# Four batches' y taken together in chunks 2 to 5, and the first quarter of w_in loaded as two column blocks, in a fused retention and GELU kernel

## The chip, the cores and the metric

The kernel runs on one core of a Trainium2 chip. The time is device microseconds of the whole kernel, from its first instruction to its last. It was measured at 217.58 us for the kernel before, the median of three runs (217.08 to 217.91).

A core has a matmul engine (TensorE, PE in the profile), two engines for elementwise work that can read the matmul results in PSUM (VectorE, DVE; ScalarE, ACT), a third [...](GpSimd, POOL), and a sequencer that only issues transfers (SyncE, SP). ScalarE and GpSimd issue transfers too. Every engine runs its own instructions in order and waits for others by semaphores.

## What is computed

The reference is a retention layer followed by a feed-forward layer. It is cut here to what matters:

```python
# attention: 4 batches, 8 heads, 768 steps, head size 64
gamma = 1.0 - 2.0 ** (-5.0 - np.arange(H))
for t in range(S):
    state = gamma * state + k[:, :, t] (outer) v[:, :, t]
    y[:, :, t] = 1/sqrt(D) * q[:, :, t] @ state
# feed-forward: x is y as (4 * 768 tokens) x 512
h = x @ w_in                       # 512 x 2048
g = 0.5 * h * (1 + tanh(c * (h + 0.044715 * h**3)))
out = g @ w_out                    # 2048 x 512
```

All inputs and the output are float32. The kernel casts to float16 for its matmuls.

## The kernel before

The kernel cuts the 768 steps into six chunks of 128 steps, numbered 0 to 5. In a chunk the recurrence becomes matmuls. With q and k scaled by powers of gamma, each batch needs:

- T: the transposes of q and k (in chunk 0 and 1 by TensorE; in chunk 2 only k by TensorE; from chunk 3 on neither: VectorE does them in blocks);
- A = k q, masked to the past, two PSUM banks per batch (64 rows of the array each);
- y = state times q ("yc"), plus v times A ("yi", 64 columns of the array each), one bank per batch;
- S = k v, which is added to the decayed state for the next chunk.

All four batches of a chunk are then one block of 512 tokens for the feed-forward layer: 16 units h (4 matmuls of 512 columns each, then a GELU on ScalarE), and 16 units o (4 matmuls of 512 columns each). While the units of chunk c run, the small matmuls of chunk c + 1 are put between them. Below, q3 means q of batch 3 in the chunk spoken of, and likewise for k and v.

The first loads. SyncE, ScalarE and GpSimd each have a queue:

```python
    nc.sync.dma_start(out=cst[:, :OKT + 16], in_=cst_h.ap())
    load1(nc.scalar, "q", 0, 0)
    load1(nc.sync, "k", 0, 0)
    load1(nc.scalar, "k", 0, 1)
    load1(nc.sync, "q", 0, 1)
    load1(nc.scalar, "v", 0, 0)
    load1(nc.sync, "v", 0, 1)
    load1(nc.sync, "k", 0, 2)
    load1(nc.sync, "q", 0, 3)
    load1(nc.sync, "v", 0, 3)
```

The scaling of one tensor, on the engine that is given:

```python
    def prep1(eng, nm, c, b):
        t = pre.tile([128, H, Dh], F16, ...)
        src = ld_tile(nm, c, b)
        if nm == "v":
            ...                                  # a cast
        else:
            eng.tensor_tensor(out=t, in0=src, in1=cst[...], op=ALU.mult)
```

PSUM has eight banks. They are given out in turn, under three tags:

```python
    BANKS = {"h": 2, "o": 2, "att": 4}

    def bank(tag, dt=F32, shape=(128, NHP, 128), name="ps"):
        return psum.tile(list(shape), dt, tag=tag, bufs=BANKS[tag], name=name)
```

The y of a pair of batches, with the A of another pair between its two parts:

```python
    def att_AY(c, bs, tag, ca, abs_, eng):
        for b in bs:
            mm_yc(c, b, tag)
        for b in abs_:
            mm_A(ca, b)
        for b in bs:
            mm_yi(c, b)
        ...                                      # ev_A and ev_Y: the copies out of PSUM
```

The first quarter of w_in comes in two halves by rows (kc 0, 1 and kc 2, 3), in a cast from float32 to float16 on the way:

```python
    NI = 4
    w_in_part = [(0, 0, 2), (0, 2, 4)] + [(i, 0, NHP) for i in range(1, NI)]
    w_in_sb = [
        const.tile([128, k1 - k0, NF // NI * 128], F16, name=f"w_in{i}_{k0}")
        for i, k0, k1 in w_in_part
    ]

    def w_in_of(fc, kc):
        i, r = fc // (NF // NI), fc % (NF // NI)
        t, k0 = (w_in_sb[i + 1], 0) if i else (w_in_sb[kc // 2], kc // 2 * 2)
        return t[:, kc - k0, r * 128:(r + 1) * 128]

    NO = 4
    w_out_sb = [const.tile([128, NF // NO, d_model], F16, name=f"w_out{i}") for i in range(NO)]

    def load_w_in(n):
        i, k0, k1 = w_in_part[n]
        nc.gpsimd.dma_start(
            out=w_in_sb[n],
            in_=moe_w_in.rearrange("(kc p) (i n) -> p kc i n", p=128, i=NI)[:, k0:k1, i],
        )
```

The start of the program, up to the point from which units of h and o run without a break (`spin` gives TensorE empty matmuls):

```python
    load1(AC, "q", 0, 2)
    load1(AC, "k", 0, 3)
    spin(14)
    prep1(VE, "q", 0, 0)

    load_w_in(0)
    prep1(PO, "k", 0, 0)
    mm_T(0, 0)
    ev_T(0, 0, AC)
    load1(AC, "v", 0, 2)
    prep1(VE, "q", 0, 1)
    prep1(PO, "k", 0, 1)
    load_w_in(1)
    prep1(PO, "k", 0, 2)
    for i in range(2, len(w_in_part)):
        load_w_in(i)
    prep1(PO, "k", 0, 3)
    for i in range(NO):
        load_w_out(i)
    spin(4)
    mm_A(0, 0)
    ev_A(0, 0)
    mm_T(0, 1)
    ev_T(0, 1, AC)
    prep1(AC, "v", 0, 0)
    spin(3)
    mm_A(0, 1)
    prep1(VE, "q", 0, 2)
    ev_A(0, 1)
    mm_yc(0, 0, "o")
    mm_yi(0, 0)
    ev_Y(0, 0, AC)
    mm_s(0, 0, "o")
    spin(3)
    prep1(AC, "v", 0, 1)
    mm_T(0, 2)
    ev_T(0, 2, AC)
    mm_yc(0, 1, "o")
    mm_yi(0, 1)
    ev_Y(0, 1, AC)
    ev_S(0, 0, AC)
    prep1(VE, "q", 0, 3)
    spin(5)
    mm_A(0, 2)
    ev_A(0, 2)


    t01, t2, t3 = (0, half), (half, half + C), (half + C, 2 * half)
    m1a = [moe1_parts(0, fp, *t01) for fp in range(2)]
    m1a[0](range(2))
    mm_T(0, 3)
    ev_T(0, 3, AC)
    m1a[1](range(2))
    mm_s(0, 1, "o")
    m1a[0](range(2, 4))
    mm_A(0, 3)
    ev_A(0, 3)
    prep1(VE, "v", 0, 2)
    m1a[1](range(2, 4))
    prep1(AC, "v", 0, 3)
    ev_S(0, 1, AC)
    mm_yc(0, 2, "o")
    mm_yi(0, 2)
    ev_Y(0, 2)
    mm_s(0, 2)
    mm_s(0, 3)
    mm_yc(0, 3, "o")
    mm_yi(0, 3)
    ev_Y(0, 3, AC)
    moe1_two(0, 0, *t2)
    moe1_two(0, 1, *t2, "o")
    moe1_two(0, 0, *t3)
    moe1_two(0, 1, *t3, "o")
```

The loads of chunk 1 (`hold` writes one element of the target when a part of w_out has landed, so that the loads behind it start no sooner), and the units between which chunk 1 is put:

```python
    hold("q", 1, 1, w_out_sb[2][0:1, 0, 0:1])
    for fc in range(4, NF):
        moe1(0, fc)
        if fc in (9, 11, 13):
            load1(AC, "qkk"[(fc - 9) // 2], 1, fc // 13)
    ...
    def preps(c, b):
        prep1(VE, "q", c, b)
        prep1(PO, "k", c, b)

    for nm, b in (("q", 1), ("q", 2), ("v", 0), ("q", 3), ("k", 3), ("v", 1), ("v", 2), ("v", 3)):
        load1(SY, nm, 1, b)
    load1(AC, "k", 1, 2)
    u = [units2(0, b, tag="ooho"[b]) for b in range(B)]
    run(
        [u[i % 3][i // 3] for i in range(12)] + u[3],
        {
            8: [(preps, 1, 0)],
            10: [(att_T, 1, 0), (preps, 1, 1)],
            11: [(prep1, AC, "v", 1, 0), (att_AY, 1, (), "att", 1, (0,), None)],
            12: [(prep1, AC, "v", 1, 1), (att_T, 1, 1), (preps, 1, 2)],
            13: [(att_AY, 1, (0,), "h", 1, (1,), AC)],
            14: [(prep1, AC, "v", 1, 2), (att_T, 1, 2), (preps, 1, 3), (att_S, 1, 0)],
            15: [
                (prep1, AC, "v", 1, 3),
                (att_AY, 1, (1,), "h", 1, (2,), AC),
                (att_T, 1, 3),
                (att_S, 1, 1),
            ],
        },
    )
```

The plan for chunk 2, and for chunks 3 to 5 (n = c + 1). The number is the unit behind which a piece stands:

```python
        {
            ...
            8: [(att_T, 2, 0), (load, 3)],
            10: [(att_T, 2, 1)],
            13: [(att_AY, 1, (), "o", 2, (0, 1), None)],
            14: [(att_T, 2, 2)],
            15: [(att_T, 2, 3)],
        },
    run(
        [x for b in range(B) for x in units2(1, b)],
        {
            2: [(att_AY, 2, (0, 1), "h", 2, (2, 3), AC)],
            4: [(att_S, 2, 0)],
            5: [(att_S, 2, 1)],
            8: [(att_AY, 2, (2, 3), "h", 2, (), AC)],
            10: [(att_S, 2, 2)],
            11: [(att_S, 2, 3)],
        },
    )


    for c in range(2, NCk - 1):
        n = c + 1
        after = {
            2: [(prep, n, 0)],
            4: [(prep, n, 1)],
            6: [(prep, n, 2), (att_T, n, 0)],
            8: [(prep, n, 3), (att_T, n, 1)],
            9: [(load, n + 1)] if n + 1 < NCk else [],
            12: [(att_AY, n, (), "att", n, (0, 1), None)],
            13: [(att_T, n, 2)],
            15: [(att_T, n, 3)],
            18: [(att_AY, n, (0, 1), "h", n, (2, 3), VE)],
            20: [(att_S, n, 0)],
            21: [(att_S, n, 1)],
            25: [(att_AY, n, (2, 3), "h", n, (), AC)],
            27: [(att_S, n, 2)],
            28: [(att_S, n, 3)],
        }
        run(
            [(lambda fc=fc: moe1(c, fc)) for fc in range(NF)]
            + [x for b in range(B) for x in units2(c, b)],
            after,
        )
```

The end of the last chunk, in two halves of 256 columns:

```python
    def moe2_last(c, b):

        hw = d_model // 2
        rows = out[b * S + c * C:b * S + (c + 1) * C, :]
        o_sb = op.tile([128, d_model], F32, tag="o", name="o_sb")
        for i in range(2):
            ps = bank("h", shape=(128, d_model), name="o_ps")
            m0, m2 = i * hw, (i + 1) * hw
            moe2_mm(ps, c, b, range(NF), m0, m2)
            nc.vector.tensor_copy(out=o_sb[:, m0:m2], in_=ps[:, m0:m2])
            nc.sync.dma_start(out=rows[:, m0:m2], in_=o_sb[:, m0:m2])
```

## Time and profile before

| What | Value |
|---|---|
| Time, median of three runs | 217.58 us |
| Span of the profiled execution | 216.2 us |
| TensorE busy (matmuls) | 206.6 us, 96% |
| TensorE weight loads | 111.7 us, 52% |
| VectorE busy | 86.7 us, 40% |
| ScalarE busy | 87.1 us, 40% |
| GpSimd busy | 96.4 us, 45% |
| Transfers | 32.79 MB, mean 152 GB/s |
| h matmuls (480) | 86.6 us |
| o matmuls (400) | 88.1 us |
| A's masking on VectorE (48) | 30.1 us, 681 ns each |

The page of a profile has six parts. The first gives how long each engine was busy. The second cuts the span into 40 equal slices, here 5.4 us each, and writes the busy share of each engine in a slice as a digit in tenths, where 9 stands for 90% or more. The third lists the transfer queues. The fourth is the chain of work that ended last: it is followed back from the last instruction, at each step to what released it or to the instruction before it on its engine. The fifth lists groups of instructions by line and shape, with the idle time before them and what ended it. The sixth lists the transfers with the time from issue to landing.

A line of the chain reads: start, length, engine, what it writes, line in the kernel. A line of the order in time reads the same, with the shapes and, in brackets, how long its engine had stood idle and for whom. All times are us from the start of the span.

### The profile page before, as it was taken

Reading aid. Unit: us, or ns where it says so; the run is one execution under the profiler, and the core shown is the slowest. Engines: PE = TensorE matmul, PEld = TensorE weight load, DVE = VectorE, ACT = ScalarE, POOL = GpSimd, SP = SyncE. Lnnn points to the kernel's source line nnn. Section 1 sums busy time; section 2 is a strip of 40 time slices with the busy share of each in tenths; the row PEclk is TensorE's granted clock in tenths of the full one; section 3 lists DMA queues with packets and bytes.
Section 4 is the critical chain, followed back from the end, with each engine's and each line's share of the span. In section 5 each row is a group of like instructions: output and inputs, shape, how many; then the busy total and the mean of one; then the engine's idle time right before and its main releaser. Section 6 shows DMA issues by size and latency. Waiting matters only on the chain.

```text
span 216.2 us, 3901 instructions
## 1 busy us (share of the span) xinstructions
PE 206.6 (96%) x1533; PEld 111.7 (52%) x1533; DVE 86.7 (40%) x155; ACT 87.1 (40%) x149; POOL 96.4 (45%) x117
## 2 busy tenths in 40 slices
PE   7785999999999999999999999999999999999992
PEld 2343644446888655444545444545444545444461
DVE  5447401068853762153691344682344650100001
ACT  2375664054455233276223275223366123475120
POOL 4578500331796242699433799411499320000000
PEclk9999999999999999999999999999999999999999
DMA  7999999998898788998769985589900012100121
GB/s 160 267 262 206 197 204 251 233 267 164 158 248 174 115 158 169 248 259 125 119 137 253 263 164 86 80 163 247 255 36 3 0 49 96 53 0 0 52 87 60
DMA packets 124290, 32.79 MB, mean 152 GB/s; under 512 B 118064, under 2 KB 122416, under 8 KB 124272
## 3 DMA queue, kind: packets, MB, share of 16 engines
q1 hardware_dynamic: 107840, 20.48, 48.2%
q0 software_dynamic: 5600, 8.65, 16.9%
q10 hardware_dynamic: 10832, 3.41, 6.4%
q8 instruction: 12, 0.20, 0.4%
q14 instruction: 6, 0.05, 0.1%
HBM read 30.44 MB, written 6.29 MB: 170 GB/s over the span
## 4 chain that ended last, share of the span: by engine, by line
PE 87%; DMA 4%; DVE 3%; SPq 2%; issue 1%; DVEq 0%
PE h_ps L422 38%; PE o_ps L467 38%; DMA q<-in_q_dram 4%; PE y_ps L307 3%; PE a_ps L272 3%; PE s_ps L326 2%; SPq L98 2%; PE y_ps L294 2%; PE qkT_ps L249 1%; DVE q L195 1%; DVE a_sb L285 1%; DVE qkT L233 0%; DVE o_sb L505 0%; DVE v L192 0%; SPq L126 0%
## 5 line engine op out<-in xcount | busy, mean ns | idle before, releaser
L467 PE MATMUL o_ps<-w_out,g 128*128 128x512 f16 (+1 forms) x400 | 88.1, 371 | 0.0
L422 PE MATMUL h_ps<-xT,w_in 128*128 128x512 f16 (+2 forms) x480 | 86.6, 337 | 0.0
L437 ACT ACTIVATE g<-h_ps 128x512 f16<-128x512 f32 (+1 forms) x98 | 57.5, 588 | 46.8 <-PE h_ps L422 46.5
L422 PEld LDWEIGHTS <-w_in 128*128 128x128 f16 x480 | 44.6, 98 | 37.3
L467 PEld LDWEIGHTS <-g 128*128 128x128 f16 x400 | 37.7, 98 | 38.8
L285 DVE TENSOR_TENSOR a_sb<-a_ps,mask 128x512 f16<-128x512 f32 x48 | 30.1, 681 | 17.0 <-PE a_ps L272 16.9
L489 ACT COPY o_sb<-o_ps 128x512 f32<-128x512 f32 x19 | 11.1, 585 | 51.1 <-PE o_ps L467 47.9
L195 POOL TENSOR_TENSOR k<-k,cst 128x512 f16<-128x512 f32 x24 | 25.0, 1047 | 14.4 <-DMA k<-in_k_dram 14.4
L494 POOL DMA_DIRECT2D out_dram<-o_sb x17 | 9.6, 568 | 48.3 <-ACT o_sb L489 38.6
L352 POOL TENSOR_TENSOR stg<-st,cst 128x512 f32<-128x512 f16 x16 | 16.5, 1042 | 15.6 <-DVE st L343 14.1
L343 DVE TENSOR_TENSOR st<-s_ps,stg 64x256 f16<-64x256 f32 x32 | 13.5, 421 | 17.8 <-PE s_ps L326 17.2
L206 POOL TENSOR_TENSOR q<-q,cst 128x512 f16<-128x512 f32 x16 | 16.6, 1044 | 0.2
L195 DVE TENSOR_TENSOR q<-q,cst 128x512 f16<-128x512 f32 x8 | 8.1, 1014 | 19.3 <-DMA q<-in_q_dram 19.3
L258 DVE STREAM_TRANSPOSE qkT<-q 128x512 f16<-128x512 f16 x16 | 11.2, 698 | 11.5 <-POOL q L206 11.4
L231 ACT CAST xT<-y_ps 128x512 f16<-128x512 f32 x15 | 8.3, 588 | 14.0 <-PE y_ps L307 14.0
L206 POOL TENSOR_TENSOR kT<-kT,cst 128x512 f16<-128x512 f32 x12 | 12.5, 1042 | 0.0
L505 DVE COPY o_sb<-o_ps 128x256 f32<-128x256 f32 x2 | 0.8, 424 | 26.6 <-PE o_ps L467 26.6
L171 PE MATMUL spin_ps<-zero 128*128 128x512 f16 x29 | 9.4, 476 | 1.3 <-DVE zero L139 1.3
L192 POOL CAST v<-v 128x512 f16<-128x512 f32 x16 | 9.7, 604 | 1.8 <-DMA v<-in_v_dram 1.8
L307 PE MATMUL y_ps<-a_sb,v 128*64 128x128 f16 x192 | 8.4, 223 | 1.3 <-DVE v L192 1.2
L272 PE MATMUL a_ps<-qkT 64*128 64x128 f16 x192 | 8.1, 218 | 1.6 <-ACT qkT L231 1.5
L258 DVE STREAM_TRANSPOSE qkT<-kT 128x512 f16<-128x512 f16 x12 | 8.3, 689 | 1.7 <-POOL kT L206 1.7
(34 smaller groups left out, 90.6 us busy)
## 6 DMA issues: line engine op xcount, KB each, us to landing
v<-in_v_dram SPq DMA_DIRECT2D x22, 256.0 KB, 4.8
k<-in_k_dram SPq DMA_DIRECT2D x19, 256.0 KB, 4.5
out_dram<-o_sb POOLq DMA_DIRECT2D x17, 256.0 KB, 3.2
q<-in_q_dram SPq DMA_DIRECT2D x64, 64.0 KB, 2.8
kT<-in_k_dram SPq DMA_DIRECT2D x48, 64.0 KB, 2.7
w_out<-in_moe_w_out_dram POOLq DMA_DIRECT2D x4, 512.0 KB, 13.6
w_in<-in_moe_w_in_dram POOLq DMA_DIRECT2D x3, 512.0 KB, 8.1
k<-in_k_dram ACTq DMA_DIRECT2D x5, 256.0 KB, 6.7
```

Of the source, the lines that this page charges most:

```text
L195: eng.tensor_tensor(out=t, in0=src, in1=cst[:, col:col + H].unsqueeze(2).broadcast_to([128, H, Dh]), op=ALU.mult,)
L206: nc.gpsimd.tensor_tensor(out=t, in0=ld_all((key, c))[:, b * NHP:(b + 1) * NHP].rearrange("p hp a d -> p (hp a) d"), in1=cst[:, col:col + ...
L258: nc.vector.transpose(out=t[:, i].rearrange("p hp t -> p (hp t)"), in_=blk16.pop((nm, c, b)).rearrange("p ha d -> p (ha d)"),)
L272: nc.tensor.matmul(out=ps[j][:, hp], lhsT=t[j * 64:(j + 1) * 64, 1, hp], rhs=t[j * 64:(j + 1) * 64, 0, hp], start=True, stop=True,)
L285: nc.vector.tensor_tensor(out=s, in0=ps[j], in1=mask[:, j], op=ALU.mult)
L307: nc.tensor.matmul(out=y_ps[j * 64:(j + 1) * 64, hp], lhsT=h16["v", c, b][:, 2 * hp + j], rhs=a_sb[c, b, j][:, hp], start=(c == 0), stop=True,
L343: eng.tensor_tensor(out=st[sl, :, b, sl], in0=s_ps[sl, :, sl], in1=stg[sl, :, b, sl], op=ALU.add,)
L352: nc.gpsimd.tensor_tensor(out=stg[:, :, b], in0=st[:, :, b], in1=cst[:, OG:OG + NHP].unsqueeze(2).broadcast_to([128, NHP, 128]), op=ALU.mult,)
L422: nc.tensor.matmul(out=out, lhsT=w_in_of(fc, kc), rhs=xT[c][:, kc, t0:t1], start=(kc == 0 and first), stop=(kc == NHP - 1), skip_group_che ...
L437: nc.scalar.activation(out=out, in_=in_, func=AF.Gelu_apprx_tanh, scale=1.0)
L467: nc.tensor.matmul(out=ps[:, n0:n1], lhsT=g_sb[c, fc // 2][:, fc % 2, b * C:(b + 1) * C], rhs=w_out_sb[fc // (NF // NO)][:, fc % (NF // NO ...
L489: nc.scalar.copy(out=o_sb, in_=ps)
```

## The change

The new kernel differs in several places at once.

- In chunks 2 to 5, the A of both pairs of batches comes first, and the y of all four batches is computed together behind it, over four banks (two of tag "h", two of tag "att"). Its copies out of PSUM are split between ScalarE and VectorE. Before, the y of each pair was a step of its own, and the A of the second pair stood inside the first. The purpose is fewer changes between kinds of matmul, and more room between a copy and what waits for it.
- The first quarter of w_in is loaded as two blocks of columns, each of which is enough for a pair of h units, in place of two halves by rows. The first is issued by GpSimd behind the scaling of k0 and k1, where the first half was issued ahead of both. With it goes the order that used the halves at the start: the first h units stand behind the fourth transpose, whole.
- On SyncE, the load of k2 stands ahead of v1.
- In chunk 0 the copy of the fourth transpose goes to VectorE, and v2 is cast ahead of the last A.
- The loads of chunk 1: v0 and v1 are issued early on ScalarE, k0 to k2 behind them, and q0 to q3 from SyncE.
- The very last copy is shared by VectorE and ScalarE.

The diff, cut to its core:

```diff
@@ the first loads
     load1(nc.scalar, "v", 0, 0)
+    load1(nc.sync, "k", 0, 2)
     load1(nc.sync, "v", 0, 1)
-    load1(nc.sync, "k", 0, 2)
@@ y of four batches
+    def att_Y(c):
+        tags = ("h", "h", "att", "att")
+        for b in range(B):
+            mm_yc(c, b, tags[b])
+        for b in range(B):
+            mm_yi(c, b)
+        for b in range(B):
+            ev_Y(c, b, (AC, VE)[b % 2])
@@ w_in
-    NI = 4
-    w_in_part = [(0, 0, 2), (0, 2, 4)] + [(i, 0, NHP) for i in range(1, NI)]
+    w_in_n = (2, 2, 4, 4, 4)
...
@@ the last copy
-            nc.vector.tensor_copy(out=o_sb[:, m0:m2], in_=ps[:, m0:m2])
+            if i == 0:
+                nc.vector.tensor_copy(out=o_sb[:, m0:m2], in_=ps[:, m0:m2])
+            else:
+                nc.vector.tensor_copy(out=o_sb[:, m0:m1], in_=ps[:, m0:m1])
+                nc.scalar.copy(out=o_sb[:, m1:m2], in_=ps[:, m1:m2])
@@ the start
     prep1(VE, "q", 0, 0)
-    load_w_in(0)
     prep1(PO, "k", 0, 0)
...
     prep1(PO, "k", 0, 1)
-    load_w_in(1)
+    load_w_in(0)
     prep1(PO, "k", 0, 2)
-    for i in range(2, len(w_in_part)):
+    for i in range(1, len(w_in_n)):
         load_w_in(i)
...
     ev_A(0, 2)
+    spin(2)
+    mm_T(0, 3)
+    ev_T(0, 3)
-    m1a = [moe1_parts(0, fp, *t01) for fp in range(2)]
-    m1a[0](range(2))
-    mm_T(0, 3)
-    ev_T(0, 3, AC)
-    m1a[1](range(2))
+    moe1_two(0, 0, *t01)
     mm_s(0, 1, "o")
-    m1a[0](range(2, 4))
     mm_A(0, 3)
+    prep1(AC, "v", 0, 3)
+    prep1(VE, "v", 0, 2)
     ev_A(0, 3)
-    prep1(VE, "v", 0, 2)
-    m1a[1](range(2, 4))
-    prep1(AC, "v", 0, 3)
...
     mm_s(0, 2)
+    moe1_two(0, 1, *t01)
     mm_s(0, 3)
@@ the loads of chunk 1
-    hold("q", 1, 1, w_out_sb[2][0:1, 0, 0:1])
+    hold("q", 1, 0, w_out_sb[2][0:1, 0, 0:1])
     for fc in range(4, NF):
         moe1(0, fc)
-        if fc in (9, 11, 13):
-            load1(AC, "qkk"[(fc - 9) // 2], 1, fc // 13)
+        if fc in (9, 11):
+            load1(AC, "v", 1, (fc - 9) // 2)
...
-    for nm, b in (("q", 1), ("q", 2), ("v", 0), ("q", 3), ("k", 3), ("v", 1), ("v", 2), ("v", 3)):
-        load1(SY, nm, 1, b)
-    load1(AC, "k", 1, 2)
+    for b in range(B):
+        load1(SY, "q", 1, b)
+    for b in range(B - 1):
+        load1(AC, "k", 1, b)
+    load1(SY, "k", 1, 3)
+    load1(SY, "v", 1, 2)
+    load1(SY, "v", 1, 3)
@@ chunk 2
-            13: [(att_AY, 1, (), "o", 2, (0, 1), None)],
-            14: [(att_T, 2, 2)],
+            13: [(att_AY, 2, (), "att", 2, (0, 1), None), (att_T, 2, 2)],
             15: [(att_T, 2, 3)],
...
-            2: [(att_AY, 2, (0, 1), "h", 2, (2, 3), AC)],
-            4: [(att_S, 2, 0)],
-            5: [(att_S, 2, 1)],
-            8: [(att_AY, 2, (2, 3), "h", 2, (), AC)],
-            10: [(att_S, 2, 2)],
-            11: [(att_S, 2, 3)],
+            1: [(att_AY, 2, (), "att", 2, (2, 3), None)],
+            4: [(att_Y, 2)],
+            6: [(att_S, 2, 0)],
+            7: [(att_S, 2, 1)],
+            8: [(att_S, 2, 2)],
+            9: [(att_S, 2, 3)],
@@ chunks 3 to 5
+            10: [(att_T, n, 2)],
             12: [(att_AY, n, (), "att", n, (0, 1), None)],
-            13: [(att_T, n, 2)],
-            15: [(att_T, n, 3)],
-            18: [(att_AY, n, (0, 1), "h", n, (2, 3), VE)],
-            20: [(att_S, n, 0)],
-            21: [(att_S, n, 1)],
-            25: [(att_AY, n, (2, 3), "h", n, (), AC)],
-            27: [(att_S, n, 2)],
-            28: [(att_S, n, 3)],
+            14: [(att_T, n, 3)],
+            17: [(att_AY, n, (), "att", n, (2, 3), None)],
+            21: [(att_Y, n)],
+            23: [(att_S, n, 0)],
+            24: [(att_S, n, 1)],
+            25: [(att_S, n, 2)],
+            26: [(att_S, n, 3)],
```

## The prediction

> **What bounds the kernel now.** I read the page's busy row and its forty slices first, then the chain of work that ended last, then the order of TensorE's work in time, and last the loads of the first 18 us one by one.
>
> ```profile
> PE 206.6 (96%) x1533; PEld 111.7 (52%) x1533; DVE 86.7 (40%) x155; ACT 87.1 (40%) x149; POOL 96.4 (45%) x117
> ...
> PE   7785999999999999999999999999999999999992
> ...
> DMA  7999999998898788998769985589900012100121
> ```
>
> TensorE is full in every slice but the first four (21.6 us) and the last. The load traffic is full just where TensorE is not. So time can be won only in the start-up, in the few us after the last matmul, and in small gaps inside the full part. The chain in order of time says what the start waits for:
>
> ```profile
> 6.03 9.41 DMA q<-in_q_dram
> ...
> 15.46 1.97 DVE q L195
> ...
> 17.48 0.62 PE qkT_ps L249 x8
> ...
> 20.92 0.35 DVE v L192
> ...
> 22.62 12.25 PE h_ps L422 x80
> ```
>
> The fourth batch's q of chunk 0 (q3) is asked for at 6.03 and is there at 15.44; VectorE then takes 1.97 us to scale it, TensorE transposes it at 17.48, and from 22.62 to the last copy at 212.27 the chain is TensorE but for some 3 us near 45 to 49. What is won before 22.6 is therefore kept, unless a later load takes the place of the wait.
>
> Why does q3 need 9.4 us? The DMA answers for short stretches give the landing of each load (issue time plus the last column):
>
> ```profile
> v<-in_v_dram SPq DMA_DIRECT2D x1, 256.0 KB, 6.9
> w_in<-in_moe_w_in_dram POOLq DMA_DIRECT2D x1, 256.0 KB, 6.8
> k<-in_k_dram SPq DMA_DIRECT2D x1, 256.0 KB, 8.1
> ...
> q<-in_q_dram ACTq DMA_DIRECT2D x1, 256.0 KB, 7.8
> ...
> w_in<-in_moe_w_in_dram POOLq DMA_DIRECT2D x1, 256.0 KB, 7.2
> ```
>
> That is: v1 issued 2.35, lands 9.25; first half of w_in 3.57, lands 10.4; k2 4.09, lands 12.2; q2 4.10, lands 11.9; second half of w_in 7.57, lands 14.8. After it come k3 (15.25), q3 (15.44), v2 (17.05), v3 (17.25). The landings nearly follow the order of issue, across the three queues. From v1 to k2 three landings take 2.95 us, about 1 us each, and the w_in half alone lands 1.15 behind v1, q2 another 1.5 behind it. So each load costs the queue some 1.2 to 1.5 us, and one taken out ahead of the others should pull the rest forward by that much; I use 1.5.
>
> **What the Trainium skill says.** "DMA: Bandwidth & Descriptors", section "Issuing engines are not separate DMA queues": loads issued from different engines run on the same DMA engines. The trace agrees, since a w_in half on GpSimd's queue stands between v1 and q2. Its section "Why a DMA increments its semaphore by 16 and not by 1" says that a load has landed only when every engine has done its part, so one late engine holds it; I count on that for q3, which lands with the traffic around it. "SBUF — State Buffer", section "SBUF: two separate sides": VectorE and GpSimd share a port pair under an exclusive lock. Agreed: scaling q takes VectorE 0.69 us alone (at 4.10) and 1.96 at 15.46, where GpSimd scales k3 from 15.79 to 16.86 and VectorE ends 0.56 after it. "TensorEngine Tiling (Array Packing)", section "Key Properties": a change of tiling mode drains TensorE. Agreed: eight yc matmuls (state times q) take 0.54 us with a change behind them (74.12 to 74.66), against 0.44 for eight s matmuls of the same size with none (0.22 for four, 77.52).
>
> **Start-up.** The new kernel issues no w_in before k0 and k1 are scaled: its first GpSimd load (two column blocks, 256 KB) takes the place that the second half has now, 7.57. On SyncE k2 changes places with v1. The ACT and SP loads of q2, k3, q3, v2, v3 keep their waits. So:
> - k2 takes v1's landing, 9.3; q2 and v1 come at about 10.4. GpSimd scales k2 by 10.4 (1.04 each) instead of 13.5, VectorE q2 by 11.1 instead of 12.6.
> - The issue of v2 on ScalarE, which occupies it from 7.25 to 10.01, and so holds the copy of the second transpose until 10.06, should shorten with the queue; I take 9.1. Everything up to A of batch 2 (now 15.46) then moves to about 14.
> - k3 and q3 land 1.5 earlier, 13.75 and 13.9. GpSimd issues four w_in loads from 10.4 to 13.5 (0.77 each) and scales k3 from 13.75 to 14.8; VectorE again ends 0.56 behind it, at 15.35, where it is 17.43 now. The fourth transpose starts 2.1 earlier.
> - Behind that transpose the old order has 5.1 us to the start of the long matmul part (17.48 to 22.56), 1.17 of it a wait for v2, which VectorE casts only after the A of batch 3. The new order casts v2 before that A, and copies the transpose on VectorE (0.69) instead of ScalarE (1.01), but behind the 1.28 us of A of batch 2; and the 16 h matmuls of 256 columns (0.11 each, 1.76) which stand partly ahead of the transpose now (0.44) all come behind it. Following it from 15.3: transpose done 15.8, h of the first pair to 16.8, s to 17.0, A waits for the copy (15.3 + 1.28 + 0.69 = 17.3) and ends 17.8, y of batch 2 18.3, s 18.5, second h pair 19.4, s 19.6, y of batch 3 (its A is through VectorE at 19.2) 20.0 to 20.1. That is 4.8 us, so 0.3 better.
> Sum: 2.4 us earlier at the point that is 22.56 now. The later weights bear this: the third w_in load lands at 19.9 now, is issued no later, and is needed at 22.
>
> **Chunk 1.** Its loads start when w_out has gone through, near 35 us, whatever TensorE does. TensorE asks for the first transpose at 44.21 now, at 41.8 then. The new order sends v0 and v1 first, then q0 and k0; from the present spacing (q0 37.1, k0 38.2, q1 39.0, q2 40.9, k1 40.9) I place k0 at 39.5 to 40.4, scaled by 41.4. Just in time. GpSimd's k scalings will meet VectorE's q1 scaling, as they do now (1.57 us at 45.53). I charge 0.4 us.
>
> **y of four batches (chunks 2 to 5).** Now: A; yc, A, yi; yc, yi, which is 2 + 3 + 2 = 7 changes of mode per chunk. Then: A; A; yc, yi: 6. A change costs about 0.11 us (0.54 - 0.44): 4 x 0.11 = 0.45 less. In chunks 3 and 4 the first s of the pair also waits now: the o matmuls before it (139.90, 8 x 0.216) end at 141.63 and it starts at 141.80, released by VectorE's A, as its bank is one of A's. With four evacuations between there is no such wait: 2 x 0.17 = 0.34 less. The matmuls themselves are the same in number, and the evacuations split over ScalarE and VectorE, neither of which is short.
> Against this: in chunk 2 the old order has a unit of h matmuls between A and the third transpose, the new one none. The transpose needs the oldest of four "att" banks, which A has just filled:
>
> ```profile
> 68.77 0.62 PE L272 MATMUL a_ps<-qkT 64*128 64x128 f16 x16
> ...
> 69.20 2.48 DVE L285 TENSOR_TENSOR a_sb<-a_ps,mask 128x512 f16<-128x512 f32 x4 [2.52 <-PE a_ps L272]
> ```
>
> VectorE frees the first bank at 69.20 + 0.62 = 69.82 (2.48 / 4), TensorE is ready at 69.33: a new wait of 0.5 us.
>
> **Tail.** The last 128 x 256 copy takes VectorE 0.42; halved over two engines, it takes 0.29 (0.42 for 256 columns and 0.69 for 512 make 0.15 fixed and 0.135 per 128): 0.13 less, if ScalarE keeps pace.
>
> Sum: -2.4 + 0.4 - 0.45 - 0.34 + 0.5 - 0.13 = -2.4 us, 215.2 us, or 1.1%.
>
> **Rivals.**
> First: the early w_in costs nothing, since the loads are shared in time and q3 lands about when it does now. GpSimd's four w_in issues, now at 10.4 and no longer behind k2's late scaling, would come between k3, q3 and v2. For it: now too the second w_in half lands just ahead of k3 and q3, which were issued before it. Against it: by 10.4 all loads on SyncE and ScalarE have been issued (the last, v3, 7.84 + 2.52). Then the start wins 0.3 to 0.8, and the total is 216.5 to 217.
> Second: the start is won, and lost at chunk 1: k0 and k1, now loaded behind v0 and v1, hold TensorE at the transposes. For it: there is under half a us of slack in my estimate, and traffic is full there. Against it: 38.2 for the second load leaves room. It would give back up to 2: 216.5 to 217.5. Should k come later still, the kernel is slower, up to 219.
> Third: the late h matmuls. If w_in's second load came behind the 512 KB ones, or h waited for it, TensorE would idle for 1 to 2 us near 18: 216.5.
> Fourth, better: TensorE, ahead of time, removes about 1 us of gaps between 44 and 54 because k2 is there sooner (now 44.4): 214.2.
>
> **Range and chances.** The two rivals that take away the gain end at 217; the better one with 0.4 more in the start ends near 213.8. Range 213.7 to 217.4. Faster by over 2% means under 213.2: 0.05. Slower by over 2% means over 221.9, which needs a wait none of these views shows: 0.03. Within 2%: 0.92.
>
> **What would show it.** q3 landing near 13.9 and the fourth transpose near 15.3; the eighty h matmuls of 128 columns starting near 20.1 instead of 22.56; the first transpose of chunk 1 near 41.8 with no wait for GpSimd's k; one gap of 0.5 us before a transpose in chunk 2; chunks 3 to 5 shorter by 0.1 to 0.3 each. I am wrong if q3 still lands after 15, or if the 2 us are gone by 54.

## The result, and the profile after

The changed kernel takes 214.56 us (median of four executions, 214.17 to 215.36) against 217.33 for the kernel before on the same chip (217.04 to 217.91): a ratio of 0.9874, with a 95% interval of 0.9837 to 0.9911. That is 2.8 us less, within 2%. The prediction was 215.2 us, in a range of 213.7 to 217.4. The two profiled executions have spans of 216.2 and 213.6 us; the steps below are read from those two. The traced execution of the changed kernel is the longest of its four (spans 213.6, 212.8, 212.8, 212.4).

The busy row and the slices of TensorE and of the transfers, changed kernel:

```profile
PE 206.3 (97%) x1535; PEld 112.1 (52%) x1535; DVE 87.5 (41%) x158; ACT 85.4 (40%) x147; POOL 97.2 (45%) x117
...
PE   7999999999999999999899999999999999999992
...
DMA  7999999999879688899789987789800012100121
```

TensorE's work is the same (206.3 us; 206.6 before). Slices 2 to 4, which stood at 7, 8 and 5, are full; a new dent stands in slice 20, near 103 us. Where each came from is seen in the chain. Its pieces in order of time, changed kernel, from 9.92 to the long run of h matmuls (start, length, engine, what it writes):

```profile
9.92 1.01 ACT qkT L231
...
10.94 0.53 ACT v L190
...
11.51 0.41 PE y_ps L307 x8
...
13.69 1.19 PE spin_ps L171 x5
14.87 0.33 PE a_ps L272 x8
15.20 0.54 PE spin_ps L171 x2
15.74 0.45 PE qkT_ps L249 x8
...
19.73 12.25 PE h_ps L429 x80
```

No load stands in it any more. The fourth transpose, at 17.48 before and released by VectorE's scaling of q3, is at 15.58 by TensorE's own order, behind A of batch 2 and two empty matmuls. The loads of that stretch, changed kernel, with the time from issue to landing in the last column:

```profile
v<-in_v_dram SPq DMA_DIRECT2D x1, 256.0 KB, 6.4
k<-in_k_dram ACTq DMA_DIRECT2D x1, 256.0 KB, 6.2
q<-in_q_dram SPq DMA_DIRECT2D x1, 256.0 KB, 6.4
```

The last of these is q3: issued at 5.73, landed at 12.13. Before it took 9.41 and landed at 15.44.

What TensorE waits for, changed kernel (total us, times, longest), and the two late waits where they stand in its order of work:

```profile
PE spin_ps L171 <- DVE zero L139: 1.3, 1, 1.3
PE a_ps L272 <- DVE qkT L258: 0.8, 1, 0.8
PE a_ps L272 <- ACT qkT L231: 0.7, 2, 0.5
PE qkT_ps L249 <- DVE a_sb L285: 0.4, 1, 0.4
```

```profile
66.50 0.38 PE L249 MATMUL qkT_ps<-iden,k 128*128 128x128 f16 x4 [0.41 <-DVE a_sb L285]
...
103.56 0.40 PE L272 MATMUL a_ps<-qkT 64*128 64x128 f16 x8 [0.79 <-DVE qkT L258]
```

The first is the new wait of chunk 2 that was predicted at 0.5. The second is the dent near 103, and was not predicted. Last, the end of the chain, changed kernel:

```profile
207.82 0.43 DVE o_sb L501
...
208.28 1.62 DMA out_dram<-o_sb
209.90 0.26 ACT o_sb L504
```

ScalarE's half of the last copy starts at 209.90; VectorE's half had started at 209.57. The chain puts ScalarE's wait down to the transfer of the first 256 columns; the part on the tail below shows that VectorE's half ended it.

Stage by stage, with stage borders taken from the first matmul of each:

| Stage (its end, before and after) | Before | After | Difference | Predicted |
|---|---|---|---|---|
| To the fourth transpose | 17.48 | 15.58 | -1.90 | -2.1 |
| From there to the h matmuls of 128 columns (22.56, 19.66) | 5.08 | 4.08 | -1.00 | -0.3 |
| To the first transpose of chunk 1 (44.21, 41.31) | 21.65 | 21.65 | 0 | 0 |
| Chunk 1, to the first h of 256 columns (53.88, 50.43) | 9.67 | 9.12 | -0.55 | +0.4 |
| From there to A of chunk 2 (68.77, 65.32) | 14.89 | 14.89 | 0 | 0 |
| A of chunk 2 to the next h of 512 columns (89.03, 86.07) | 20.26 | 20.75 | +0.49 | +0.39 |
| Chunk 3 (121.18, 118.89) | 32.15 | 32.82 | +0.67 | -0.28 |
| Chunk 4 (153.32, 150.74) | 32.14 | 31.85 | -0.29 | -0.28 |
| Chunk 5 (184.40, 181.70) | 31.08 | 30.96 | -0.12 | -0.11 |
| The last o matmuls, and the tail | 31.80 | 31.90 | +0.10 | -0.13 |
| Sum | | | -2.60 | -2.4 |

So the sum is right to 0.2 us, and four of its terms are not: the start and chunk 1 are better by 0.5 and 0.95, the four-batch y and the tail worse by about 1.0 and 0.2.

One thing in the first row is not the change's work. The 14 empty matmuls at the very beginning took 5.51 us in the traced execution before and 6.13 in the one after, so the changed kernel's first transpose came 0.60 later (7.20, 6.60). In the traces of e7_tail_one and e12_three below, which are the same program up to there, they took 4.82 and 4.95, and the fourth transpose came at 14.53 and 14.88.

### The profile page after: what moved, and what is told of

Read it like the earlier page. It is cut to its first block, busy times and chain, and to the rows that moved or that the text cites. A ratio compares the mean times of both kernels' runs of the same rounds, so it can differ in the third digit from the quotient of the medians.

```text
span 213.6 us, 3916 instructions
## 1 busy us (share of the span) xinstructions
PE 206.3 (97%) x1535; PEld 112.1 (52%) x1535; DVE 87.5 (41%) x158; ACT 85.4 (40%) x147; POOL 97.2 (45%) x117
## 4 chain that ended last, share of the span: by engine, by line
PE 93%; DVE 2%; ACT 1%; DMA 1%; issue 0%
PE h_ps L429 39%; PE o_ps L462 38%; PE spin_ps L171 4%; PE y_ps L307 3%; PE a_ps L272 3%; PE qkT_ps L249 2%; PE s_ps L326 2%; PE y_ps L294 2%; DVE a_sb L285 1%; ACT qkT L231 1%; DMA out_dram<-o_sb 1%; DVE qkT L258 1%; ACT v L190 0%; DVE o_sb L501 0%; DVE zero L139 0%
## 5 line engine op out<-in xcount | busy, mean ns | idle before, releaser
L195 POOL TENSOR_TENSOR k<-k,cst 128x512 f16<-128x512 f32 x24 | 25.8, 1081 | 12.6 <-DMA k<-in_k_dram 12.6
L195 DVE TENSOR_TENSOR q<-q,cst 128x512 f16<-128x512 f32 x8 | 6.3, 793 | 21.5 <-DMA q<-in_q_dram 21.5
L233 DVE CAST xT<-y_ps 128x512 f16<-128x512 f32 x11 | 7.2, 685 | 11.4 <-PE y_ps L307 11.4
L171 PE MATMUL spin_ps<-zero 128*128 128x512 f16 x31 | 10.6, 493 | 1.3 <-DVE zero L139 1.3
L231 ACT CAST xT<-y_ps 128x512 f16<-128x512 f32 x13 | 7.2, 588 | 9.3 <-PE y_ps L307 9.3
L482 DVE COPY o_sb<-o_ps 128x512 f32<-128x512 f32 x4 | 2.8, 692 | 19.0 <-PE o_ps L462 14.7
```

Of the source, the lines that this page charges most:

```text
L171: nc.tensor.matmul(out=ps, lhsT=zero[:, 0:128], rhs=zero, start=True, stop=True)
L195: eng.tensor_tensor(out=t, in0=src, in1=cst[:, col:col + H].unsqueeze(2).broadcast_to([128, H, Dh]), op=ALU.mult,)
```

## The experiments

The theory after the result: the start is won by w_in's halves, which no longer stand ahead of q2, k2 and q3 in the queues (1.9 us), and by the order behind the fourth transpose (1.0 us). The y of four batches, which the title names first, is worth next to nothing. The rivals: k2's exchange with v1 wins the start; or the y of four wins in chunks 2 to 5 and something else loses there. Each time below is a median, and each ratio is against the kernel before, run on the same chip on the same occasion (medians 217.45, 217.40 and 217.29 us).

| Kernel | Time, us | Ratio, 95% interval |
|---|---|---|
| e1_w_late | 216.57 | 0.9983 (0.9961 to 1.0005) |
| e2_k2_first | 221.84 | none |
| e3_w_early | 215.68 | 0.9923 (0.9909 to 0.9938) |
| e4_y_only | 217.18 | 0.9984 (0.9968 to 0.9999) |
| e5_t2_back | 213.96 | 0.9826 (0.9797 to 0.9855) |
| e6_qk_first | 214.99 | 0.9883 (0.9855 to 0.9912) |
| e7_tail_one | 214.19 | 0.9841 (0.9816 to 0.9867) |
| e8_less_spin | 214.66 | 0.9868 (0.9833 to 0.9903) |
| e9_all | 213.99 | 0.9841 (0.9807 to 0.9876) |
| e10_v2_ahead | 215.17 | 0.9905 (0.9877 to 0.9933) |
| e11_k2_w_behind | 217.40 | 1.0001 (0.9980 to 1.0021) |
| e12_three | 214.30 | 0.9844 (0.9804 to 0.9884) |

### Where the start's gain comes from

**e1_w_late**, the kernel before with only the two w_in halves issued later:

```diff
-    load_w_in(0)
     prep1(PO, "k", 0, 0)
...
     prep1(PO, "k", 0, 1)
-    load_w_in(1)
+    load_w_in(0)
     prep1(PO, "k", 0, 2)
-    for i in range(2, len(w_in_part)):
+    for i in range(1, len(w_in_part)):
```

> The kernel before with one thing moved: the first half of w_in is issued behind the scaling of k1 (where its second half was), the second half behind the scaling of k2. Theory (the early w_in half stands in the queue ahead of k2 and q2, the second one ahead of the end of k3 and q3): q3 lands near 12.5 instead of 15.44, the fourth transpose starts near 15.3, the long stretch of h matmuls of 128 columns starts 2.0 to 2.4 us sooner than 22.56, and the whole is 215.0 to 215.6. Rival (the order of TensorE's and VectorE's work around the fourth transpose, or the exchange of k2 and v1, made the gain): q3 lands where it did, the start moves by less than 0.7, the whole is above 216.8.

It takes 216.57 us, less won than expected, and the interval of its ratio reaches past 1: in time the gain is not shown. Its trace (span 214.1) shows q3 landed at 12.0, where it was 15.44 before, and the fourth transpose at 15.61, where the changed kernel has it (15.58), with k2 and v1 in the old order: so the place of the w_in loads alone gives the first part. The second part is missing, since the 128-column h matmuls start at 20.91, not 19.66. The one wait in between, in TensorE's order of work of this kernel:

```profile
19.66 0.41 PE L307 MATMUL y_ps<-a_sb,v 128*64 128x128 f16 x8 [1.39 <-DVE v L192]
```

It is not v2's load that is late. VectorE casts v2 behind the last A, at 18.97, because the old order puts it there. Of twenty executions thirteen had spans of 214.1 to 215.0 at a mean TensorE clock of 0.996 or more, and seven had spans of 216.0 to 216.9 at 0.981 to 0.991. So the median stands for less than the trace shows (214.1 against 216.2 before).

**e10_v2_ahead** mends that alone, on top of e1_w_late:

```diff
+    prep1(VE, "v", 0, 2)
     ev_A(0, 3)
-    prep1(VE, "v", 0, 2)
```

> The kernel before with its two w_in halves issued late (as e1_w_late) and v2 cast by VectorE ahead of the last A of chunk 0 instead of behind it. Theory, that the second part of the start's gain in the changed kernel is this order alone: the 1.4 us wait of y for v2 is gone, the eighty h matmuls start at 19.4 to 19.8 (20.91 in e1_w_late), the fourth transpose stays at 15.6, the time is about 1 us below e1_w_late's: 215.2 to 215.8. Rival, that the h matmuls' new place or the VectorE copy of the transpose bring it: the start at 20.4 to 20.9, no gain.

The time is 215.17, 1.4 below e1_w_late's median and 1.0 below the median of its thirteen executions at the higher clock (216.19); here no execution is at a clock under 0.996. So in time the order of v2's cast is worth about what the theory said. The trace, however, does not show the start expected (19.4 to 19.8): it is at 21.29. In TensorE's order of work of this kernel the wait for v2 is gone, and others stand in its place:

```profile
15.72 0.40 PE L249 MATMUL qkT_ps<-iden,k 128*128 128x128 f16 x4 [0.70 <-POOL k L195]
...
17.95 0.61 PE L422 MATMUL h_ps<-xT,w_in 128*128 128x256 f16 x4 [1.18 <-DMA w_in<-in_moe_w_in_dram]
...
20.63 0.38 PE L326 MATMUL s_ps<-v,k 128*128 128x128 f16 x4 [0.52 <-ACT v L190]
```

The second half of w_in by rows is needed by the very first pair of h units; issued at 11.57, it landed at 17.9, late for that. This is what the blocks by columns are for: the first block alone serves the first pair, and the second is wanted one pair later, at 18.12 in the changed kernel, which shows no wait for w_in at all. The traced execution is one of the longest two of its eight (spans 213.2 to 214.4); how often the wait for w_in comes is open. No kernel had the column blocks alone, so what they are worth in time was not tested.

**e3_w_early** is the opposite test: the changed kernel with its first w_in block issued ahead of k0, as before.

```diff
     prep1(VE, "q", 0, 0)
+    load_w_in(0)
     prep1(PO, "k", 0, 0)
...
-    load_w_in(0)
     prep1(PO, "k", 0, 2)
```

> The kernel after with only its first w_in block (256 KB, two column blocks of 128) issued ahead of the scaling of k0, where the kernel before issues its first half. Theory: q3 lands 1.3 to 2 us later than the 12.13 of after; TensorE, which bounds the start of after by its own order, feels only part of it: the 128-column h matmuls start 0.5 to 1.5 us later than 19.66, the whole is 215.1 to 216.1. Rival (order of work on TensorE and VectorE made the gain): less than 0.3 us, the whole within 214.3 to 214.9.

As expected: 215.68 us, a ratio of 0.9923 where the changed kernel has 0.9874 (the two intervals just meet at 0.991). q3 lands at 13.8 instead of 12.13, so one load of 256 KB ahead of it costs it 1.7 us. The h matmuls of 128 columns start at 21.12 instead of 19.66, with waits of 0.29, 0.46 and 0.28 before them, one of them for v3. So the early w_in block costs some 1.1 us of the total.

**e2_k2_first** and **e11_k2_w_behind** test the other half of the loads' order, k2 ahead of v1, in the kernel before. In e2 it is all that changes; in e11 the three 512 KB loads of w_in come behind k3's scaling besides:

```diff
+    load1(nc.sync, "k", 0, 2)
     load1(nc.sync, "v", 0, 1)
-    load1(nc.sync, "k", 0, 2)
... e11 only
+    prep1(PO, "k", 0, 3)
     for i in range(2, len(w_in_part)):
         load_w_in(i)
-    prep1(PO, "k", 0, 3)
```

> The kernel before with only k2 and v1 exchanged on SyncE's queue. Theory of the early w_in: as many bytes stand ahead of q3 as before, so q3 lands within 0.5 of 15.44 and the start of the 128-column h matmuls moves by less than 0.5 from 22.56; the whole is 216.8 to 217.8. k2 lands near 10.5 instead of 12.2 and its transpose waits no more for GpSimd. Rival (the exchange is what counts): the start moves by 1 us or more, the whole is below 216.5.

> The kernel before with k2 and v1 exchanged (as e2_k2_first) and the three 512 KB loads of w_in issued behind k3's scaling. Theory, that e2_k2_first lost because those loads were issued early and stood ahead of v2 and v3: v2 lands at 16 to 17.5, the waits of 3.1 and 1.4 us are gone, the clock doesn't fall, the eighty h matmuls start at 21.5 to 22.3, time 216.3 to 217.2. Rival, that the exchange itself delays v2 and v3: v2 still lands near 22, and the time stays near 221.

Neither wins. Of four executions of e2 one took 216.81 us and three 221.84 to 222.69, too far apart for a ratio; the trace is of one of the three. In it v2, issued at 7.27 on ScalarE's queue, landed 14.7 us later, beside w_in loads that GpSimd had issued from 9.73 to 12.0, and TensorE waited 3.06 us for it. In e11 these loads are issued from 16.05, v2 lands 9.6 after its issue, and none of twelve executions is above 218.38. This agrees with the Trainium skill, "DMA: Bandwidth & Descriptors", section "Queues, rings and completion order", by which a transfer engine takes turns between the queues that have work; it follows that a load issued earlier is slowed by one that joins later on another queue. That this is the whole cause in e2 was not shown. With those loads held back the exchange wins no time: e11 has a ratio of 1.0001, although its fourth transpose came 0.77 sooner (16.71) and its h matmuls 0.44. So the exchange is not what won the start. What it adds beside late w_in loads, as in the changed kernel, was not tested.

### The y of four batches

**e4_y_only** is the kernel before with only the new plan of chunks 2 to 5:

```diff
-            13: [(att_AY, 1, (), "o", 2, (0, 1), None)],
-            14: [(att_T, 2, 2)],
+            13: [(att_AY, 2, (), "att", 2, (0, 1), None), (att_T, 2, 2)],
...
-            18: [(att_AY, n, (0, 1), "h", n, (2, 3), VE)],
+            17: [(att_AY, n, (), "att", n, (2, 3), None)],
+            21: [(att_Y, n)],
... and the rest of both plans, and att_Y
```

> The kernel before with only the named part of the change: the y of all four batches together in chunks 2 to 5, with its plan of units; start, loads of chunk 1 and the end as before. Theory: this part alone brings nothing. Chunk 2 loses 0.45 (a wait of the third transpose for VectorE), chunks 3 to 5 win 0.29 + 0.29 + 0.12, and as TensorE is not ahead of the loads here, the wait of 0.8 in chunk 3 does not come: 217.0 to 217.4, chunk 3 (89 to 121) near 31.85. Rival (the wait of chunk 3 belongs to the new order of A, not to loads that come late): chunk 3 takes 32.5 or more and the whole is at or above 217.6.

It gives 0.9984, at most 0.7 us. The trace has chunk 2 at 20.75 (+0.49, with a wait of 0.56 before the third transpose) and chunks 3 to 5 at 31.85, 31.86 and 30.96 (-0.30, -0.28, -0.12), a sum of -0.21; predicted were -0.29. There is no wait in chunk 3. So the wait of 0.79 there is not made by the new plan alone.

**e5_t2_back** puts the third transpose of chunk 2 back by one unit in the changed kernel, which takes its wait away:

```diff
-            13: [(att_AY, 2, (), "att", 2, (0, 1), None), (att_T, 2, 2)],
+            13: [(att_AY, 2, (), "att", 2, (0, 1), None)],
+            14: [(att_T, 2, 2)],
```

> The kernel after, with the third transpose of chunk 2 put back behind one unit of h matmuls (unit 14). Theory: the wait of that transpose for VectorE (0.41 in after) goes, chunk 2 (from its first A to the first h of 512 columns) takes 20.75 - 0.45 = 20.3 us. As TensorE is then still further ahead of the loads of chunk 3, the wait there grows by about as much, and the whole stays at 214.3 to 214.7. Rival (the wait in chunk 3 is a fixed consequence of the order of work on VectorE): it stays 0.8, and the whole falls by 0.45 to 214.1.

Chunk 2 falls from 20.75 to 20.16, and chunk 3 rises from 32.82 to 33.14, in TensorE's order of work of this kernel:

```profile
103.26 0.40 PE L272 MATMUL a_ps<-qkT 64*128 64x128 f16 x8 [1.11 <-DVE qkT L258]
```

Half of what chunk 2 wins is waited for in chunk 3: A of its second pair stands nearly still (103.56, 103.26), whatever comes before. The time, 213.96, is the lowest of all the runs, but its interval and the changed kernel's overlap.

What holds that A? VectorE's order of work in the changed kernel:

```profile
99.21 0.71 DVE L258 STREAM_TRANSPOSE qkT<-kT 128x512 f16<-128x512 f16 x1 [0.30 <-POOL kT L206]
99.85 2.44 DVE L285 TENSOR_TENSOR a_sb<-a_ps,mask 128x512 f16<-128x512 f32 x4
102.22 0.69 DVE L258 STREAM_TRANSPOSE qkT<-q 128x512 f16<-128x512 f16 x1
102.83 0.67 DVE L258 STREAM_TRANSPOSE qkT<-kT 128x512 f16<-128x512 f16 x1
```

A's four copies come first, and the last transposes of q and k behind them. But the last one could not have come sooner: GpSimd scaled its k^T until 102.75, and it began at 102.83. GpSimd's own order of work, changed kernel:

```profile
92.00 1.04 POOL L195 TENSOR_TENSOR k<-k,cst 128x512 f16<-128x512 f32 x1 [2.06 <-DMA k<-in_k_dram]
...
101.70 1.05 POOL L206 TENSOR_TENSOR kT<-kT,cst 128x512 f16<-128x512 f32 x1
```

From 92.00 to 102.75 GpSimd works without a break, one tensor behind the other. Before that it stood for 2.06 us on a load of chunk 3, k of batch 0; the transfers are busy to 80% or more in nearly every slice up to there. In the kernel before, that load had landed in time, and the same scaling began at 92.89 without a wait. So TensorE entered the stretch 2.96 us sooner (86.07, 89.03), but GpSimd's row of scalings began only 0.89 sooner.

**e6_qk_first** lets GpSimd scale q and k^T of all four batches first in chunk 3, and the k and v that TensorE needs later behind them:

```diff
+        if n == 3:
+            after.update({
+                2: [(blk, n, 0, 1), (att_T, n, 0)],   # blk: q and k^T alone
+                4: [(blk, n, 2), (att_T, n, 1)],
+                6: [(blk, n, 3), (att_T, n, 2)],
+                8: [(flat, n, 0, 1, 2, 3)],           # flat: k and v
+                10: [],
+            })
```

> The kernel after, with GpSimd's scalings for chunk 3 in another order: q and the transposed k of all four batches first, then k and v, so that the late k0 (92.0) does not stand ahead of the q and k that the transposes need. Theory: the wait of A for VectorE's transposes in chunk 3 (0.79) goes, chunk 3 takes 31.85 instead of 32.82, the whole is 213.4 to 213.8. Rival (VectorE or the banks hold the second A): the wait stays, the whole is 214.3 or more.

The mechanism holds: the wait is gone and chunk 3 is 31.86. The total is not better, 214.99. In chunk 2 two waits stand now, in TensorE's order of work of this kernel:

```profile
66.40 0.40 PE L272 MATMUL a_ps<-qkT 64*128 64x128 f16 x8 [0.43 <-DVE qkT L233]
66.99 0.38 PE L249 MATMUL qkT_ps<-iden,k 128*128 128x128 f16 x4 [0.20 <-DVE a_sb L285]
```

These lie ahead of the edit, so the edit did not make them; the traces of e7 and e8, which share nothing with it but the changed kernel, show the same pair (0.35 or 0.39, and 0.20). And e3, e7 and e8 have no wait in chunk 3 without any edit there. The landing of that one load accounts for it. In the traces of the changed kernel, e5, e7 and e8 the scaling of k of batch 0 waits for it and begins at 92.00, 91.70, 91.18 and 90.32, and in all four the last transpose ends 11.5 us later, at 103.50, 103.21, 102.69 and 101.83. In the first two TensorE waits there, 0.79 and 1.11 us; in the last two it begins the second half of A at 102.77 and 102.22, behind that end, and does not wait. So less than a microsecond in one load decides whether the wait is there. How often it is there in executions that were not traced stays open.

### The tail and the empty matmuls

**e7_tail_one** leaves the last copy whole on VectorE:

```diff
-            if i == 0:
-                nc.vector.tensor_copy(out=o_sb[:, m0:m2], in_=ps[:, m0:m2])
-            else:
-                nc.vector.tensor_copy(out=o_sb[:, m0:m1], in_=ps[:, m0:m1])
-                nc.scalar.copy(out=o_sb[:, m1:m2], in_=ps[:, m1:m2])
+            nc.vector.tensor_copy(out=o_sb[:, m0:m2], in_=ps[:, m0:m2])
```

> The kernel after, with the last copy whole on VectorE as in the kernel before. Theory: ScalarE's share of the last copy waits for the transfer of the first half (it starts 0.33 behind VectorE's), so the split costs 0.2 instead of winning 0.13: the stretch from the last matmul to the end falls from 4.06 to 3.9, the whole by 0.1 to 0.2. Rival (the split wins what was predicted): it grows by 0.13.

From the last matmul to the end it takes 3.86 us instead of 4.06; the last copy ends 0.45 behind that matmul instead of 0.63. The end of its chain has no transfer in it:

```profile
203.95 4.80 PE o_ps L462 x38
...
208.77 0.42 DVE o_sb L500
```

So the split costs 0.2 us where 0.13 was to be won. The two halves in the changed kernel's order of work:

```profile
209.57 0.29 DVE L503 COPY o_sb<-o_ps 128x128 f32<-128x128 f32 x1 [1.32 <-PE o_ps L462]
209.90 0.27 ACT L504 COPY o_sb<-o_ps 128x128 f32<-128x128 f32 x1 [3.23 <-DMA out_dram<-o_sb]
```

The mark puts ScalarE's wait down to the transfer of the first 256 columns, as the theory did. But that transfer, issued at 208.28, took 1.7 us to land, until about 210.0, when ScalarE's half had begun. What had just ended is VectorE's half, at 209.86, and the trace has ScalarE's half wait for a semaphore that VectorE's raises. In e5, e6 and e8, too, it begins 0.03 to 0.04 us behind the end of VectorE's. So the halves run one after the other, 0.29 + 0.27 where the whole copy takes 0.42. Both write one tile and read one bank; which of these makes the program wait was not tested.

The total, 214.19, is lower by more than 0.2. This execution started sooner: its first 14 empty matmuls took 4.82 us, where they took 6.13 in the changed kernel's trace, and the fourth transpose came at 14.53. The Trainium skill, "TensorE: Matmul & The Clock Gate", section "Part 1: The HAM clock gate (the "warmup" mystery)", says that the window after which the full clock is granted runs freely, so that the slow phase of one kernel differs between executions. These two traces fit that: an empty matmul takes 0.63 us at first in both, and 0.38 us in e7 from about 4 us on, while in the changed kernel's trace those near 6 us are still slow (the clock in the profile reads 1.00 in both all the while). So 1 us of difference at the start of two single traces says nothing of the two kernels. Nor did it last: the first transpose of chunk 1 stands at 41.24 in e7 and at 41.31 in the changed kernel. The shorter span of e7 (212.6, 213.6) is the missing wait in chunk 3 (31.85 instead of 32.82) and the tail.

**e8_less_spin** takes 9 empty matmuls away (12, 4, 3, 0, 3, 0 in place of 14, 4, 3, 3, 5, 2), since TensorE's own order now holds the fourth transpose (the text below says ten).

> The kernel after with ten empty matmuls left out at the start (14, 4, 3, 3, 5, 2 become 12, 4, 3, 0, 3, 0). Theory: in after the fourth transpose waits for no load but for TensorE's own order, empty matmuls included; it comes about 1.0 us sooner than 15.58, and so does the start of the 128-column h matmuls (near 18.7). The wait in chunk 3 takes most of it back: the whole is 214.0 to 214.6. Rival (loads or ScalarE hold the start): the start moves by less than 0.4. A second rival: the clock granted to TensorE falls without the empty matmuls, and the h matmuls of the start take longer.

The transpose comes at 13.62 and the h matmuls at 18.86, 0.8 sooner than in the changed kernel's trace. But e7, with all its empty matmuls, has 14.53 and 18.85. Beside it the 0.9 at the transpose is gone by the h matmuls, as TensorE waits 0.61 for VectorE's cast of v2 in between. The total is 214.66, no gain. In the trace 0.39 is waited for at A of chunk 2, and the span is 212.2, but the other executions reach 213.7.

**e9_all** joins e5, e6, e7 and e8 (with all nine empty matmuls taken away; the text below counts seven), and **e12_three** joins the first three of them:

> The changed kernel with four small edits at once: the third transpose of chunk 2 back one unit, q and k^T of all four batches scaled ahead of k and v in chunk 3, the last copy whole on VectorE, and 7 empty matmuls fewer at the start. Theory: each removes a wait that was seen (0.4 us in chunk 2, 0.8 to 1.1 in chunk 3, 0.2 in the tail, 0.8 in the start), but chunk 2 hands part of the start's gain back as a wait of up to 0.5 at its first A, since its loads come no earlier. Profiled span 211.0 to 212.3, median 213.0 to 213.9, chunk 3 31.86 with no wait, tail 3.86. Rival, that what is won anywhere ahead of chunk 3 is fully taken back by its loads: median as the changed kernel, 214.2 to 214.8.

> The changed kernel with three of those edits, and all its empty matmuls. Theory: chunk 2 about 20.2 to 20.6, chunk 3 31.86 without a wait, tail 3.86; 0.6 to 1.2 below the changed kernel, median 213.3 to 213.9, and e9_all at most 0.5 below this one. Rival, that the start decides: e9_all 0.8 below this one. Rival, that the loads decide: both at 214.2 to 214.8.

Both have the waits of chunk 3 removed (31.85, 31.86), as the theory said, and e9 chunk 2 at 20.16. The tail is 3.95. The times, 213.99 and 214.30, do not bear the theory out: the first lies between its range and that of the rival that the loads decide, the second within the rival's. Neither is shown to be faster than the changed kernel, whose ratio interval overlaps both, nor than each other. Where e9's sooner start (18.63, by 1.03) went, is in its order of work:

```profile
41.17 0.40 PE L249 MATMUL qkT_ps<-iden,q 128*128 128x128 f16 x4 [0.45 <-DVE q L195]
```

The first transpose of chunk 1 waits for q, and stands at 41.17, 0.14 sooner than in the changed kernel. In e12 the same wait is 0.83, and in e7 it is 0.57. Chunk 1's loads are held back until the third part of w_out has landed (34.49 in e9, 33.91 in the changed kernel, 32.91 before), so they follow the transfers and not TensorE: the scaling of q begins 5.9 to 6.2 us behind that landing in the changed kernel, e7, e8, e9 and e12. This is the prediction's second rival, for q and not for k. No fixed time says when it binds: in e8, where the part landed at 33.71, the transpose stood at 40.66 without a wait, and in e12, with 34.96, at 41.74 with one.

## Why the prediction was right, and where it was not

The time was right, and so was that it stays within 2%, but in part by luck: two stretches came out 1.45 us better than said and two 1.25 worse, and these cancel. Step by step:

**The fourth transpose, 2.1 us earlier: right in size (1.90), for a reason that holds only half.** The mechanism, w_in out of the way of q3, is shown by e1_w_late. The mis-sized term is "k3 and q3 land 1.5 earlier": q3 landed 3.31 earlier, at 12.13. One load was counted as taken out ahead of it, and there were two, since the second half (landed at 14.8) also came in ahead of q3. With q3 scaled at 13.31, the load was no longer what held the transpose: TensorE's own work, empty matmuls included, held it to 15.58. The sign "q3 near 13.9" was missed for that reason. The price of one load was sized nearly right: 1.5 was set, and e3_w_early shows 1.7.

**Behind the transpose, 0.3 better: in fact 1.00.** The order was followed rightly, to 4.8 us, and it took 4.08. A of batch 3 was said to wait for VectorE's copy, 2.0 behind the transpose; it started 1.64 behind it without a wait, as VectorE had taken A of batch 2 0.34 ahead of the transpose. The A and the two y matmuls behind it took 0.33 to 0.34 each on the path, where 0.4 to 0.5 were set. That v2 must be cast ahead of the last A was named, and e10_v2_ahead bears it out in the time (1.0 to 1.4 us), though not in its trace.

**Chunk 1, a charge of 0.4: wrong in sign, -0.55.** The charge was for GpSimd's k meeting VectorE's q. Before, q1 was scaled by VectorE in 1.57 us at 45.53; after, in 0.87 at 42.64. The better rival, which takes gaps out of 44 to 54, came true by half, and not for its reason: k2 was scaled from 44.64, no sooner than before (44.51). Which of the changes made q1's scaling short was not tested.

**y of four batches: right alone, not in company.** The step "four mode changes less, two waits of 0.17 less, one wait of 0.5 more" made -0.29, and e4_y_only measures -0.21 in the trace. The price of a mode change, 0.11, fits chunk 5, which has only that and is 0.12 shorter. In the changed kernel it came to +0.75 in chunks 2 to 5, chiefly for one reason that no step had: the wait of 0.79 in chunk 3. The prediction followed the loads to chunk 1 and no further, though the slices showed the transfers nearly full as far as there.

**Tail, -0.13: wrong, +0.10.** The proviso "if ScalarE keeps pace" failed: its half began only behind the end of VectorE's, 0.33 after that had started.

**The rivals.** The first (q3 no earlier) and third (h waits for w_in) fell for the changed kernel; e10_v2_ahead shows the third in a kernel without column blocks. The second did not bind in the changed kernel (41.31, no wait), but did in three variants with a sooner start.

In time, the parts add up roughly: w_in later and v2's cast, 0.9905 (e10_v2_ahead); the y of four, 0.9984 (e4_y_only); the product is 0.9889, of 0.9874. So some three quarters of the gain are the loads' order and one cast, and the y of four batches is worth 0.16% by itself (0.01 to 0.32). The rest is within the noise; the column blocks, the new loads of chunk 1 and the copy of the fourth transpose on VectorE have no run of their own.

## What to carry to other kernels

When the start of a kernel waits for a load, count every load that lands ahead of it, also those issued behind it; and look next at what the vector engines do in between, as one cast in the wrong place was here worth about as much as the loads. Where the transfers are full for the first half of a kernel, time won by TensorE ahead of them is lent: the next loads take part of it back, at a place that shifts with what was won. Dividing a copy over two engines can lose where the second half waits for the first. And when a profile names what ended a wait, check that it had ended by then.

## What the runs showed of the hardware

- Of two scalings side by side on VectorE and GpSimd, either can be the one that is held. Scaling q3 took VectorE 1.96 us before and 0.68 after; in exchange GpSimd's scaling of k3 beside it took 1.59 us instead of 1.07. VectorE had begun at 12.63, GpSimd at 12.61. The prediction had VectorE lose again. Both times the one that was held had begun first by the trace, by 0.33 us (15.46, 15.79) and by 0.02.
- The clock fell behind a wait of TensorE. In the traced execution of e2_k2_first TensorE was busy for 1.17 of the 5 us from 20 to 25; the granted clock was 0.81 there and 0.51 in the next 5 us, in which TensorE was busy for 4.92, and the run of 80 h matmuls took 14.09 us (25.81 to 39.90) instead of 12.15 in the kernel before (22.56 to 34.71). In these three stretches of that kernel the columns are the stretch and its length, the busy time of TensorE, its weight loads, VectorE, ScalarE and GpSimd, then the clock, the time of the transfers' packets as a share of the 16 transfer engines, and GB/s:

```profile
20.00:25.00 5.00, 1.17 (x16) 0.85 (x16) 2.04 (x5) 1.09 (x4) 0.18 (x1) 0.81 1.23 202
25.00:30.00 5.00, 4.92 (x45) 4.24 (x44) 0.84 (x2) 2.31 (x6) 3.04 (x3) 0.51 1.24 206
30.00:35.00 5.00, 5.00 (x25) 2.29 (x24) 0.00 (x0) 3.06 (x6) 0.18 (x1) 1.00 1.15 192
```

  So in that execution the run behind the wait took 1.94 us longer than it did before, on top of the wait.
- Column blocks of w_in took the transfers more time. The first quarter comes in 1024 packets of 512 bytes, at 59.5 ns each, and as row halves it came in 512 packets of 1024 bytes, at 98 ns: 60.9 against 50.2 us of packet time, or 0.67 us on each of 16 engines. w_out's third part landed 1.0 us later (33.91 against 32.91), but hardly for that: in e3_w_early, with the same blocks, it landed at 33.12.
